# Attention with routing into eight experts: another order of work where the last attention units meet the first expert blocks

## The chip, the cores and the metric

One core of a Trainium2 chip runs one program. The metric is the device time of one execution in microseconds (us). Instructions of the five engines are named PE (TensorE matmul), PEld (TensorE weight load), DVE (VectorE), ACT (ScalarE), POOL (GpSimd) and SP (SyncE, which here only issues DMAs).

## What is computed

Attention with capped scores over 4 batches of 12 heads, 448 rows and 64 columns, then a layer of eight experts in which each of the 1792 rows goes to the one expert with its largest gate logit:

```python
scores = cap * np.tanh(scale * np.matmul(q, k.transpose(0, 1, 3, 2)) / cap)
attn = np.exp(scores - np.max(scores, axis=-1, keepdims=True))
attn = attn / (np.sum(attn, axis=-1, keepdims=True) + 1e-09)
x = np.matmul(attn, v)           # 4 batches, heads side by side: x is 1792 x 768
e_idx = np.argmax(x @ w_gate, axis=1)
gate_w = softmax(x @ w_gate)[np.arange(N), e_idx]
eom = 1 / (1 + np.exp(-(x @ w_output_gate)))
for e in range(8):
    mask = e_idx == e
    h = np.maximum(x[mask] @ w1[e], 0.0)          # 768 x 1024
    out[mask] = gate_w[mask, None] * eom[mask, e, None] * (h @ w2[e])   # 1024 x 768
```

## The kernel before, in words

**Attention.** The work is cut into 24 units, `u` = 0 to 23; a unit is two heads of one batch, six units a batch. A unit has four score steps `qk(u, 0..3)` on PE, each followed on ACT by a tanh (`th`, L302) and an exponential (`pt`, L284). One unit later come the value products `pv(u, 0..3)` (L317, L320) into the PSUM tile `u`, and `u_evac` (L338 on ACT or L340 on DVE, chosen by unit number) copies that to `ut`. The sums of the exponentials are added up by `presum` (L328, L329, L333: `pa`, `pb`), on POOL for units 0 to 21 and on DVE for units 22 and 23; `sums` (L352) then reduces two units at a time over partitions on PE. `t_k` and `t_q` (L271, L258: `tk`, `tq`) turn the keys and queries two units ahead, and DVE makes their low parts `KL`, `QL` (L252).

**End of a batch.** When a batch's units are done, `end_of_batch` normalises, routes and stores its rows: `row_tr(p)` turns a unit's result on PE (`trow`, L483), `row_out(p)` scales it on DVE (`xr`, L487) and sends it to the DRAM tensor `xs`, and `place`, `enter` and so on enter each row's position in the tables `tab`, with an indirect DMA on POOL (L474). The tiles `tk`, `tq`, `trow` and most other turned tiles share one tag of two PSUM buffers (`ps_t`, tag "t"), so that each waits until DVE or ACT has read the tile two before it.

**The seam.** For the first three batches the steps are hung into the score loop by a table of positions (`at`: four positions a unit, counted from the batch's end; for the third batch 7 is the last quarter of unit 20, 9 and 10 lie in unit 21, 15 and 16 in the last quarter of unit 22 and the first of unit 23). `RWP` holds the positions of the rows 1 to 5 of the third batch; row 0 stands at 6. `NXP` holds those of the six steps of `early()`, which work out on DVE, in operations on one partition, which expert (`meta` row 0), whether it changes (row 1) and which table range (row 2) each of the first five expert blocks has. Step 5 is the seven operations from `bval` to the second `meta`, step 6 the four from `bch` to `used`. `fetch_dma(i)` (L733) has SP read four table pieces `tc` for block `i`, `gather(i)` adds them up on POOL (L738 to L741) and fetches the block's 128 rows of `xs` by an indirect DMA (`xg`, L748), and `tx(i)` turns these on PE (`pt_x`, L760), with `xh` and `xl` made by ACT and DVE. `load_raw` (L710) has SP load one 512 KB or 384 KB piece of an expert's weights. The first blocks use only rows of the first three batches.

**Experts.** Blocks 0 and 1 go through the same weights together (`mm_two`), chunk by chunk of 128 input columns; a chunk is six matmuls for each block (L968). Each weight piece is first split by ACT (L946) and DVE (L947) into a high and a low part. The rest of the last batch's routing is a list of steps, `STEPS`, one group taken after each chunk (`step()` in `between`): `g` and `G` are the gate products, `s` reads the sums, `S` turns them, `x`, `X`, `l`, `c`, `r`, `p`, `q`, `e` route, digits are rows, `n` is a step of `late()`, `zh` fetches the next block's tables.

**What sets the order.** The program is written out by hand, and each engine runs its part of it strictly in that order. SP's DMAs use eight semaphores in turn, so that each DMA waits until the eighth before it has landed.

Of the kernel before, what the change touches and what calls it, by code (L numbers as in the profile page):

```python
# [21 lines left out]
def tile_kernel(ctx: ExitStack, tc, q, k, v, cap, w_gate, w_ogate, w1, w2, out):  # L22
    nc = tc.nc
    B, H, S, D = q.shape
# [5 lines left out]
    NU = B * NP  # L30
    REG = 15 * 128
    NTAB = 128 + E * REG
    NSLOT = 18
    NE = 5
# [16 lines left out]
    AH = 6  # L51
    PZ = 4
    RWP = (9, 10, 12, 13, 14)
    NXP = (7, 7, 7, 7, 7, 7)
    F1 = 5
    F2 = 4
    PRE = 3
    STEPS = 'g s S G x0 X1 l2 c rp3 n4 n5 q e n n n n n n zh'
    WARM = (32, 8, 12, 0)
    RB = 7  # L60
    SP0 = 3
# [2 lines left out]
    UACT = 18  # L64
# [269 lines left out]

    def u_evac(u):
        t = utp.tile([128, S], F32, tag="ut", name="ut")
        if UACT <= u < NU - 2 or u == NU - 1:
            nc.scalar.activation(out=t, in_=ups.pop(u), func=ACTF.Copy)  # L338
        else:
            nc.vector.tensor_copy(out=t, in_=ups.pop(u))  # L340
        ut[u] = t

    def sums(u):

        b, p = divmod(u, NP)
        if p % 2 == 0:
            return
        r = p // 2
        if r == 0:
            smt[b] = ps_m.tile([128, S], F32, tag="sm", name="sm")  # L350
        for g in range(4):
            nc.tensor.matmul(smt[b][32 * g:32 * g + 32], lhsT=ohc[:, r, :], rhs=s1[u - 1 + g // 2][:, g % 2],  # L352
                             start=(r == 0), stop=(r == NP // 2 - 1))
# [10 lines left out]
    def end_of_batch(b):  # L364
# [128 lines left out]
        L = lambda *fs: (lambda: [f() for f in fs])  # L493
        P = lambda f, *a: (lambda: f(*a))
# [3 lines left out]
        if b < B - 2:  # L498
            at = {1: [t[2], t[3]], 2: [sums_out], 5: [t[1]], 6: [rws[0]], 9: [gts[0]], 10: [rws[1]], 13: [gts[1]], 14: [rws[2]],
                  15: [logits], 16: [choose], 18: [rws[3]], 21: [rank_mm, place], 22: [rws[4]], 23: [place2], 24: [enter]}  # L500
            at.setdefault(26 if b < B - 3 else 22, []).append(rws[5])
        elif b == B - 2:
            g = early()
            nx = P(next, g, None)
            lds = [P(load_raw, 0, w, c) for w in range(2) for c in range((KD, KF)[w])]
            fd = [P(fetch_dma, i) for i in range(NE)]
            at = {-1: [sums_out], 1: [t[2], t[3]], 2: [t[1], *gts], 3: [logits], 4: [choose],
                  6: [rws[0]], 6.5: [rank_mm, place, place2, enter]}
            for i, x in enumerate(RWP, 1):
                at.setdefault(x, []).append(rws[i])  # L510
            for i, x in enumerate(NXP):
                at.setdefault(x, []).append(nx)
            for x, fs in ((10.5, [fd[0], fd[1], P(set_known, NE), lds[0]]), (15, [P(gather, 0), *lds[1:6], fd[2]]),
                          (16, [P(gather, 1), fd[3], *lds[6:]])):
                at.setdefault(x, []).extend(fs)
        if b < B - 1:
            for x, fs in at.items():
                for f in fs:
                    slots.setdefault(4 * NP * (b + 1) + 4 + x, []).append(f)
            return  # L520
        nx = P(next, late_steps, None)
        do = dict(g=t[2], s=t[0], S=t[1], G=t[3], x=gts[0], X=gts[1], l=logits, c=choose, r=rank_mm, p=place, q=place2,
                  e=enter, n=nx, z=L(P(set_known, NSLOT), P(fetch_dma, NE)), h=lambda: next(rests(), None))
        do.update({str(p): rws[p] for p in range(NP)})
        return [L(*[do[x] for x in w]) for w in STEPS.split()]


    def M(nm, shape):
        return rtp.tile(shape, F32, tag="b" + nm, name="b" + nm)

    def red(o, i, op=ALU.add):
        nc.vector.tensor_reduce(out=o, in_=i, axis=AX.X, op=op)

    def tt(o, x, y, op):
        nc.vector.tensor_tensor(out=o, in0=x, in1=y, op=op)
# [51 lines left out]
    def early():  # L587


        cnt, key, srt, gt = M("cnt", [1, E]), M("key", [1, E]), M("srt", [1, E]), M("le", [1, E, E])  # L590
        cm, nb, nbp, more = M("cm", [1, E]), M("nb", [1, E]), M("nbp", [1, E]), M("more", [1, E])
        g14 = M("g14", [1, E, 14])
        lo, hi = M("lo", [1, 1, E]), M("hi", [1, 1, E])
        tt(cnt, pres[(B - 1) % 2][0:1, 0], ereg, ALU.subtract)

        stt(srt, cnt, float(E), ALU.mult, e8, ALU.subtract)
        ts(cm, cnt, -127.0, ALU.add)
        tt(gt, over(srt, E), srt.unsqueeze(2).to_broadcast([1, E, E]), ALU.is_gt)
        tt(g14, cm.unsqueeze(2).to_broadcast([1, E, 14]), mrow.unsqueeze(1).to_broadcast([1, E, 14]), ALU.is_gt)
        red(key, gt)  # L600
        red(nb, g14)
        yield

        ts(nbp, key, 0.0, ALU.is_equal, 2.0, ALU.mult)
        ts(more, key, float(E - 1), ALU.is_equal, float(NE), ALU.mult)
        tt(nbp, nbp, nb, ALU.max)
        tt(gt, over(key, E), key.unsqueeze(2).to_broadcast([1, E, E]), ALU.is_le)
        tt(nbp, nbp, more, ALU.add)
        yield
        tt(gt, gt, over(nbp, E), ALU.mult)  # L610
        red(hi[:, 0], gt)
        tt(lo[:, 0], hi[:, 0], nbp, ALU.subtract)
        yield
        yield from slots_of(lo, hi, nb, ereg.unsqueeze(1), 0, NE)
# [60 lines left out]
    def rests():  # L675

        full, h, hx, wo = rt["rest"]
        sh = [1, 2, NO, E]
        oh, o2 = M("roh", sh), M("ro2", sh)
        two = lambda x: x.unsqueeze(2).to_broadcast(sh)  # L680
        own = lambda i: metah[:, i, NW:].rearrange("a (z n) -> a z n", z=2)
        tt(wo, wo, over(full, NW), ALU.mult)
        tt(oh, two(hx), irow[:, 0:NO].unsqueeze(1).unsqueeze(3).to_broadcast(sh), ALU.is_equal)
        red(metah[:, 2, 0:NW], wo, ALU.max)
        tt(oh, oh, two(h), ALU.mult)
        tt(o2, oh, full.unsqueeze(1).unsqueeze(1).to_broadcast(sh), ALU.mult)
        red(own(1), oh, ALU.max)
        red(own(2), o2, ALU.max)
        tt(o2, oh, e8.unsqueeze(1).unsqueeze(1).to_broadcast(sh), ALU.mult)
        red(own(0), o2, ALU.max)  # L690
        yield


    tb, xg = {}, {}
# [38 lines left out]
            nc.sync.dma_start(out=t4[:, c], in_=tabs[c][bass.ds(off, 128)])  # L733

    def gather(i):
        t4 = tcs.pop(i)
        t = xgp.tile([128, 2], F32, tag="tb", name="tb", bufs=6)
        nc.gpsimd.tensor_tensor(out=t4[:, 0:2], in0=t4[:, 0:2], in1=t4[:, 2:4], op=ALU.add)  # L738
        nc.gpsimd.tensor_tensor(out=t, in0=t4[:, 0], in1=t4[:, 1], op=ALU.add)
        ti = xgp.tile([128, 1], U32, tag="ti", name="ti", bufs=6)  # L740
        nc.gpsimd.tensor_scalar(out=ti, in0=t[:, 0:1], scalar1=float(NT), scalar2=None, op0=ALU.add)  # L741
        tb[i] = (t, ti)
        n = (B - 1) * S if i < NE else NT + 8
        g = xgp.tile([128, DM], F32, tag="xg", name="xg")
        if i in (1, 3, 4):

            nc.gpsimd.memset(g, 0.0)
        nc.gpsimd.indirect_dma_start(  # L748
            out=g, out_offset=None, in_=xs[0:n], in_offset=bass.IndirectOffsetOnAxis(ap=ti, axis=0),
            bounds_check=n - 1, oob_is_err=i not in (1, 3, 4))  # L750
        xg[i] = g

    def tr_split(src, n, tag, bufs, pool):
        hi = pool.tile([128, n, 128], F32R, tag=tag + "h", name=tag + "h", bufs=bufs)
        lo = pool.tile([128, n, 128], F32R, tag=tag + "l", name=tag + "l", bufs=bufs)
        for a in range(0, n, 4):
            m = min(4, n - a)
            ps = ps_t.tile([128, 4, 128], F32, tag="t", name="pt_" + tag)
            for c in range(m):
                nc.tensor.transpose(ps[:, c], src[:, (a + c) * 128:(a + c + 1) * 128], ident)  # L760
            nc.scalar.activation(out=hi[:, a:a + m], in_=ps[:, 0:m], func=ACTF.Copy)
            nc.vector.tensor_tensor(out=lo[:, a:a + m], in0=ps[:, 0:m], in1=hi[:, a:a + m].bitcast(F32), op=ALU.subtract)
        return hi, lo

    def tx(i):
        if i < NSLOT:
            xg[i] = tr_split(xg[i], KD, "x", 2, xgp)
# [58 lines left out]
    for b in range(B - 1):  # L826
        end_of_batch(b)

    def step():
        if bg:  # L830
            bg.pop(0)()
# [28 lines left out]
    for u in range(NU):  # L860
# [24 lines left out]
        if u > 0:  # L885
            pv(u - 1, 3)
            u_evac(u - 1)
# [8 lines left out]
    u = NU - 1  # L896
# [245 lines left out]

    split_to(SP0)
    bg.extend(end_of_batch(B - 1))
    pv(u, NK)
    u_evac(u)
    tx(0)
    step()
    sums(u)
    step()  # L1150
    gather(2)

    def last_bg():
# [20 lines left out]
    for k in range(NH):  # L1174
        i = SIDES[k][0]
# [69 lines left out]
```

## Time and profile before

| | us |
|---|---|
| median of 3 runs (lowest to highest) | 529.62 (529.43 to 530.06) |
| the profiled execution, its own time | 527.99 |
| its span, first to last instruction | 526.3 |
| PE busy in the span | 508.1 (97%) |
| granted TensorE clock, mean | 0.995 of full speed |
| ACT, DVE, POOL busy | 381.6, 345.5, 298.7 |

PE is busy nearly all the time, so the table says little by itself: what matters is the few stretches in which PE is idle or runs slowly, and what it waits for there. The profile's time is 1.6 us under the median, of which 1.7 us lie around the span.

### The profile page before, as it was taken

The page shows a single profiled execution, that of the slowest core. Times are in us where ns is not written, and L with a number is a line of the kernel's source. Part 1 is how long each engine was busy: PE and PEld are TensorE (multiplying, and loading weights), DVE is VectorE, ACT ScalarE, POOL GpSimd, SP SyncE. Part 2 cuts the span into 40 slices and gives each one's busy share as a digit, 9 for nine tenths or more (in the row PEclk, how much of TensorE's full clock was granted, in tenths as well). Part 3 has the DMA queues.
Part 4 walks back from the last instruction along what each step waited for, and adds up shares of the span by engine and source line. Part 5 has one row for each costly group of instructions (what it writes and reads, how often), then busy time and mean ns, then how long its engine had stood idle before and what let it go on. Part 6 is the DMA issues. An engine that isn't in the chain of part 4 may idle for free. (4 is left out here: it accounts for less than half of the span.)

```text
span 526.3 us, 10342 instructions
## 1 busy us (share of the span) xinstructions
PE 508.1 (97%) x3197; PEld 361.5 (69%) x3197; DVE 345.5 (66%) x576; ACT 381.6 (73%) x498; POOL 298.7 (57%) x341
## 2 busy tenths in 40 slices
PE   7999999999999989699999999999999999999995
PEld 6555465555655544377999898887878968666692
DVE  3363354965496877599998996975758686545460
ACT  5989897888787978535678886886766787555561
POOL 8988967778987696435254975314737015182001
PEclk9999999999999999899999999999999999999999
DMA  6644434445445316887159636329659959994001
GB/s 148 142 108 102 105 74 106 103 108 111 102 113 132 73 36 189 289 303 219 49 184 389 243 95 206 128 69 386 242 169 391 375 173 368 359 349 167 1 31 49
DMA packets 106189, 91.94 MB, mean 175 GB/s; under 512 B 80770, under 2 KB 88970, under 8 KB 106128
## 3 DMA queue, kind: packets, MB, share of 16 engines
q1 hardware_dynamic: 97392, 58.48, 38.2%
q0 software_dynamic: 8736, 32.74, 17.2%
q8 instruction: 27, 0.44, 0.3%
q14 instruction: 34, 0.28, 0.2%
HBM read 123.68 MB, written 12.04 MB: 258 GB/s over the span
## 5 line engine op out<-in xcount | busy, mean ns | idle before, releaser
L947 DVE TENSOR_TENSOR wr<-raw,wr 128x768 fp32r<-128x768 f32 (+1 forms) x167 | 172.0, 1067 | 68.3 <-ACT wr L946 59.4
L946 ACT ACTIVATE wr<-raw 128x768 fp32r<-128x768 f32 (+1 forms) x167 | 150.2, 936 | 33.0 <-DMA raw<-in_moe_w_dram 12.1
L302 ACT ACTIVATE th<-s,icap 128x896 f32<-128x896 f32 x96 | 84.3, 915 | 27.4 <-PE s L297 19.0
L284 ACT ACTIVATE pt<-th,capc 128x896 f32<-128x896 f32 x96 | 85.7, 947 | 0.0
L968 PE MATMUL py<-wr,hh 128*128 128x384 f32 x352 | 77.3, 340 | 0.0
L968 PE MATMUL php<-wr,xh 128*128 128x512 f32 x264 | 74.8, 404 | 0.0
L1037 POOL DMA_INDIRECT out_dram<-yo,ti x13 | 18.5, 1426 | 86.6 <-ACT yo L1035 62.2
L968 PEld LDWEIGHTS py<-wr,hh 128*128 128x128 f32 x352 | 61.2, 188 | 4.0 <-issue 3.7
L317 PE MATMUL u<-pt,vv 128*64 128x448 f32 x288 | 59.4, 548 | 0.5 <-ACT ut L338 0.5
L968 PEld LDWEIGHTS php<-wr,xh 128*128 128x128 f32 x264 | 47.6, 189 | 12.9 <-issue 2.1
L329 POOL TENSOR_TENSOR pb<-pa,pt 128x896 f32<-128x896 f32 x22 | 46.5, 2113 | 17.0 <-issue 13.7
L333 POOL TENSOR_TENSOR pb<-pb,pt 64x448 f32<-64x448 f32 x44 | 52.1, 1185 | 4.5 <-DMA tab<-ent,posi 1.2
L328 POOL TENSOR_TENSOR pa<-pt 128x896 f32<-128x896 f32 x22 | 46.3, 2104 | 2.3 <-ACT ex L439 0.8
L968 PE MATMUL py<-wr,hl 128*128 128x384 f32 x176 | 44.8, 335 | 0.0
L968 PE MATMUL php<-wr,xl 128*128 128x512 f32 x132 | 41.4, 395 | 0.0
L317 PEld LDWEIGHTS u<-pt,vv 128*64 128x64 f32 x288 | 18.5, 136 | 30.5 <-issue 23.1
L1084 POOL DMA_DIRECT2D rh<-in_moe_w_dram x42 | 23.5, 561 | 22.7 <-issue 16.3
L297 PE MATMUL s<-QH,KH 64*128 64x448 f32 x144 | 31.7, 432 | 1.7 <-ACT th L302 1.7
L968 PEld LDWEIGHTS py<-wr,hl 128*128 128x128 f32 x176 | 31.8, 188 | 0.0
L340 DVE COPY ut<-u 128x448 f32<-128x448 f32 x19 | 11.8, 623 | 29.9 <-PE u L320 29.1
L968 PEld LDWEIGHTS php<-wr,xl 128*128 128x128 f32 x132 | 24.7, 187 | 6.0
L1138 POOL DMA_INDIRECT out_dram<-yh,toh x6 | 6.0, 1008 | 38.0 <-ACT wr L946 10.0
(243 smaller groups left out, 862.6 us busy)
## 6 DMA issues: line engine op xcount, KB each, us to landing
raw<-in_moe_w_dram SPq DMA_DIRECT2D x78, 512.0 KB
raw<-in_moe_w_dram SPq DMA_DIRECT2D x104, 384.0 KB
rh<-in_moe_w_dram POOLq DMA_DIRECT2D x18, 512.0 KB
rh<-in_moe_w_dram POOLq DMA_DIRECT2D x24, 384.0 KB
lq<-in_q_dram SPq DMA_DIRECT2D x24, 224.0 KB
kk<-in_k_dram SPq DMA_DIRECT2D x24, 192.0 KB
vv<-in_v_dram SPq DMA_DIRECT2D x24, 192.0 KB
xs<-xr SPq DMA_DIRECT2D x18, 224.0 KB
```

The lines of the kernel that those rows point to most:

```text
L284: nc.scalar.activation(out=dst, in_=th, func=ACTF.Exp, scale=capc)
L297: nc.tensor.matmul(ps[:, j, 0:S], lhsT=x[h, sl], rhs=y[h], start=(i == 0), stop=(i == 2))
L302: nc.scalar.activation(out=th[:, 0:n], in_=ps[:, 0:n, 0:S], func=ACTF.Tanh, scale=icap)
L317: nc.tensor.matmul(ups[u][64 * j:64 * j + 64], lhsT=V[:, c, j, :], rhs=P[:, 2 * c + j], start=(c == 0), stop=False)
L328: eng.tensor_tensor(out=a, in0=P[:, 0:2], in1=P[:, 2:4], op=ALU.add)
L329: eng.tensor_tensor(out=s1[u], in0=a, in1=P[:, 4:6], op=ALU.add)
L333: eng.tensor_tensor(out=s1[u][h, j], in0=s1[u][h, j], in1=P[h, 2 * NK], op=ALU.add)
L946: nc.scalar.activation(out=t[:, 0, 0:F], in_=raw, func=ACTF.Copy)
L947: nc.vector.tensor_tensor(out=t[:, 1, 0:F], in0=raw, in1=t[:, 0, 0:F].bitcast(F32), op=ALU.subtract)
L968: nc.tensor.matmul(ps[g][:, 0:n], lhsT=st[:, c], rhs=w[:, z, g * n:(g + 1) * n], start=(c == 0 and st is hi and z == 0), stop=(c == (KD, K ...
L1037: nc.gpsimd.indirect_dma_start(out=out, out_offset=bass.IndirectOffsetOnAxis(ap=ti, axis=0), in_=y, in_offset=None, bounds_check=NT - 1, o ...
L1084: nc.gpsimd.dma_start(out=d, in_=src[bass.ds(e, 1)].rearrange("e (k p) f -> p (e k) f", p=128)[:, c], **kw)
```

## The change

The diff moves work; no computation is added or dropped. `gather` is split into `index` (the additions) and `take` (the indirect DMA).

```diff
-    NXP = (7, 7, 7, 7, 7, 7)
+    NXP = (7, 7, 7, 7, 9, 10)
-    STEPS = 'g s S G x0 X1 l2 c rp3 n4 n5 q e n n n n n n zh'
+    STEPS = 'g U s S G x0 X1 l2 c 3r p4 n5 n q e nn n n nn zh'
 def u_evac(u):
-        if UACT <= u < NU - 2 or u == NU - 1:
+        if UACT <= u < NU - 3 or u == NU - 1:
 # end_of_batch, third batch
-            for x, fs in ((10.5, [fd[0], fd[1], P(set_known, NE), lds[0]]), (15, [P(gather, 0), *lds[1:6], fd[2]]),
-                          (16, [P(gather, 1), fd[3], *lds[6:]])):
+            for x, fs in ((10.5, [fd[0], P(set_known, NE)]), (11, [lds[0], P(index, 0)]), (14, [fd[1]]),
+                          (15, [P(take, 0), fd[2], *lds[1:4]]), (16, [P(gather, 1), *lds[4:6], fd[3], *lds[6:]]),
+                          (18.5, [P(tx, 0)])):
 # end_of_batch, last batch
-                  e=enter, n=nx, z=...
+                  e=enter, n=nx, U=P(sums, NU - 1), z=...
     def gather(i):
+        index(i)
+        take(i)
+
+    def index(i):
         ...
         tb[i] = (t, ti)
+
+    def take(i):
+        ti = tb[i][1]
         n = (B - 1) * S if i < NE else NT + 8
 # after the loop over units
     pv(u, NK)
     u_evac(u)
-    tx(0)
-    step()
-    sums(u)
     step()
     gather(2)
```

On PE, where attention ends (`vv_129` belongs to unit 22, `vv_130` to unit 23; `php` is chunk 0), before:

```order
L320 MATMUL u<-pt,vv_129 128x448
L317 MATMUL u<-pt,vv_130 64x448 x6
L320 MATMUL u<-pt,vv_130 128x448
L760 MATMUL pt_x<-ident,xg 128x128 x6
L389 MATMUL tg<-ut,wg 32x448 x4
L352 MATMUL sm<-pb,ohc 32x448 x4
L968 MATMUL php<-wr,xh 128x512 x4
L968 MATMUL php<-wr,xl 128x512 x2
```

And now:

```order
L320 MATMUL u<-pt,vv_129 128x448
L768 MATMUL pt_x<-ident,xg 128x128 x6
L317 MATMUL u<-pt,vv_130 64x448 x6
L320 MATMUL u<-pt,vv_130 128x448
L389 MATMUL tg<-ut,wg 32x448 x4
L976 MATMUL php<-wr,xh 128x512 x4
L976 MATMUL php<-wr,xl 128x512 x2
L352 MATMUL sm<-pb,ohc 32x448 x4
```

The turning of the gathered rows now stands ahead of unit 23's value products, and the last sums behind chunk 0.

On DVE, in unit 21, before (from the end of step 5 on):

```order
L535 TENSOR_TENSOR bo_2452<-bo_2452,boh 1x40
L532 TENSOR_REDUCE meta<-bo_2452 1x5
L535 TENSOR_TENSOR bch<-meta 1x4
L532 TENSOR_REDUCE bsm<-boh 1x4
L535 TENSOR_TENSOR meta<-bch,bsm 1x4
L532 TENSOR_REDUCE used<-boh 1x8
L487 TENSOR_TENSOR xr<-trow,rec 112x512 x2
L252 TENSOR_TENSOR KL<-tk,KH 128x512
L252 TENSOR_TENSOR QL<-tq,QH 128x448
```

And now (between the first rows and the last, the middle of step 5 is left out):

```order
L487 TENSOR_TENSOR xr<-trow,rec 112x512
L543 SCALAR_TENSOR_TENSOR bval<-blo,ereg 1x8
...
L536 TENSOR_TENSOR bo_2452<-bo_2452,boh 1x40
L533 TENSOR_REDUCE meta<-bo_2452 1x5
L487 TENSOR_TENSOR xr<-trow,rec 112x512
L536 TENSOR_TENSOR bch<-meta 1x4
L533 TENSOR_REDUCE bsm<-boh 1x4
L536 TENSOR_TENSOR meta<-bch,bsm 1x4
L533 TENSOR_REDUCE used<-boh 1x8
L252 TENSOR_TENSOR KL<-tk,KH 128x512
L252 TENSOR_TENSOR QL<-tq,QH 128x448
```

Step 5 moved from ahead of both rows to between them, step 6 to behind the second row and ahead of `KL`.

On SP, in units 21 to 23, with the semaphores that each DMA waits for (`raw_0` and `raw_1` are the first two weight pieces, `xs` the rows 3 to 5), before:

```order
L710 DMA raw_0_112<-in_moe_w_dram 128x1024 [waits DMAHW5_49]
L110 DMA vv_130<-in_v_dram 128x6x64 [waits DMAHW6_49,PE_49]
L112 DMA vv_130<-in_v_dram 64x64 [waits DMAHW7_49,PE_49]
L112 DMA vv_130<-in_v_dram 64x64 [waits DMAHW0_49]
L490 DMA xs<-xr 448x1x128 [waits DMAHW1_49,DVE_49]
L490 DMA xs<-xr 448x1x128 [waits DMAHW2_49,DVE_49]
L490 DMA xs<-xr 448x1x128 [waits DMAHW3_49,DVE_49]
L710 ISA
L710 DMA raw_1_113<-in_moe_w_dram 128x1024 [waits DMAHW4_49]
```

And now (the four pieces of block 1's table and some register work are left out):

```order
L711 DMA raw_0_112<-in_moe_w_dram 128x1024 [waits DMAHW4_49]
L490 DMA xs<-xr 448x1x128 [waits DMAHW5_49,DVE_49]
L490 DMA xs<-xr 448x1x128 [waits DMAHW6_49,DVE_49]
L490 DMA xs<-xr 448x1x128 [waits DMAHW7_49,DVE_49]
...
L734 DMA tc<-tab_108 128x2 [waits DMAHW4_49]
L734 ISA
L734 DMA tc<-tab_109 128x2 [waits DMAHW5_49]
L734 ISA
L734 DMA tc<-tab_110 128x2 [waits DMAHW6_49]
L734 ISA
L734 DMA tc<-tab_111 128x2 [waits DMAHW7_49]
L711 ISA
L711 DMA raw_1_113<-in_moe_w_dram 128x1024 [waits DMAHW0_49]
```

The pieces 1 to 5 of the first weights, which followed the rows directly, now follow eight table reads of blocks 1 and 2, and the last four of these wait on the semaphores of `raw_0` and the rows.

## Rows read from the trace of the kernel before

**Rows 1.** Stages: us, busy (x count) of five engines, PEclk, DMA share, GB/s

```profile
216.10:220.40 4.30, 4.28 (x23) 1.59 (x24) 1.02 (x2) 1.58 (x4) 1.50 (x4) 0.60 0.45 134
...
400.00:500.00 100.00, 100.00 (x577) 73.39 (x576) 60.82 (x67) 63.56 (x86) 31.91 (x46) 1.00 0.72 268
```

**Rows 2.** PE at the seam: start, us, instruction, idle before and releaser

```profile
208.33 2.48 PE L317 MATMUL u<-pt,vv 128*64 128x448 f32 x12
210.74 1.02 PE L320 MATMUL u<-pt,vv 128*128 128x448 f32 x2
216.12 0.85 PE L760 MATMUL pt_x<-ident,xg 128*128 128x128 f32 x6 [4.36 <-DMA xg<-xs,ti]
216.89 1.72 PE L389 MATMUL tg<-ut,wg 128*32 128x448 f32 x8
218.38 1.73 PE L352 MATMUL sm<-pb,ohc 128*32 128x448 f32 x8
220.03 1.32 PE L968 MATMUL php<-wr,xh 128*128 128x512 f32 x4
221.66 0.60 PE L372 MATMUL trec<-ident,ssb 128*112 128x128 f32 x4
```

**Rows 3.** PE, the same forms at full clock elsewhere

```profile
205.08 0.96 PE L352 MATMUL sm<-pb,ohc 128*32 128x448 f32 x8
```

**Rows 4.** SP: start, us of issuing, DMA and count

```profile
203.06 1.98 SPq L490 DMA_DIRECT2D xs<-xr  x3
205.26 3.31 SPq L710 DMA_DIRECT2D raw<-in_moe_w_dram  x5
```

**Rows 5.** POOL, units 20 to 23

```profile
190.77 2.09 POOL L329 TENSOR_TENSOR pb<-pa,pt 128x896 f32<-128x896 f32 x1
192.94 2.35 POOL L333 TENSOR_TENSOR pb<-pb,pt 64x448 f32<-64x448 f32 x2
195.37 2.11 POOL L328 TENSOR_TENSOR pa<-pt 128x896 f32<-128x896 f32 x1
199.74 4.33 POOL L333 TENSOR_TENSOR pb<-pb,pt 64x448 f32<-64x448 f32 x2
209.00 1.14 POOL L748 DMA_INDIRECT xg<-xs,ti  x1 [3.43 <-DMA raw<-in_moe_w_dram]
```

**Rows 6.** DMA queues in 209.0 to 213.0: packets, MB, share of 16 engines

```profile
q1 hardware_dynamic: 393, 1.45, 98.3%
```

**Rows 7.** DVE, PE and ACT in units 21 and 22

```profile
187.14 0.15 DVE L542 SCALAR_TENSOR_TENSOR bval<-blo,ereg 1x8 f32<-1x8 f32 x1
188.67 2.04 DVE L535 TENSOR_TENSOR meta<-bch,bsm 1x4 int32<-1x4 f32 x1
190.77 1.27 DVE L487 TENSOR_TENSOR xr<-trow,rec 112x512 f32<-112x512 f32 x2
...
186.88 0.65 PE L483 MATMUL trow<-ident,ut 128*112 128x128 f32 x4
...
192.09 0.60 PE L258 MATMUL tq<-ident,lq 112*128 112x112 f32 x4
...
194.35 0.65 PE L483 MATMUL trow<-ident,ut 128*112 128x128 f32 x4 [0.25 <-DVE KL L252]
...
189.63 1.53 ACT L302 ACTIVATE th<-s,icap 128x896 f32<-128x896 f32 x2 [2.80 <-PE s L300]
```

**Rows 8.** DVE, then POOL, in another batch's end

```profile
149.84 2.15 DVE L542 SCALAR_TENSOR_TENSOR cand<-d,iota 112x32 f32<-112x32 f32 x1
...
149.83 2.11 POOL L328 TENSOR_TENSOR pa<-pt 128x896 f32<-128x896 f32 x1
```

**Rows 9.** DVE in unit 22

```profile
200.02 1.08 DVE L328 TENSOR_TENSOR pa<-pt 128x896 f32<-128x896 f32 x1
```

**Rows 10.** PE's waits from 220 to the end: us in total, times, longest

```profile
PE trow L483 <- DVE bcm L542: 0.7, 1, 0.7
```

**Rows 11.** PE's wait in unit 23

```profile
202.68 2.48 PE L317 MATMUL u<-pt,vv 128*64 128x448 f32 x12 [0.53 <-ACT ut L338]
```

More of the change, by code (lines that the diff above doesn't have):

```diff
@@ L522, in end_of_batch @@
         do = dict(g=t[2], s=t[0], S=t[1], G=t[3], x=gts[0], X=gts[1], l=logits, c=choose, r=rank_mm, p=place, q=place2,
-                  e=enter, n=nx, z=L(P(set_known, NSLOT), P(fetch_dma, NE)), h=lambda: next(rests(), None))
+                  e=enter, n=nx, U=P(sums, NU - 1), z=L(P(set_known, NSLOT), P(fetch_dma, NE)), h=lambda: next(rests(), None))
         do.update({str(p): rws[p] for p in range(NP)})
```

## The prediction

> **What bounds the kernel now.** I read the stages first: from 400 to 500 us PE is busy all the time at full clock [rows 1], and it is so over nearly the whole expert part. There a start that is earlier by one us ends the kernel one us earlier, so the change is worth what it moves the point at which the expert part gets going. As that mark I take the end of chunk 0, 221.66 in PE's rows [rows 2], with turned rows, unit 23's value products, the gate products of one group and the last sums done.
>
> PE's rows at the seam show what is lost ahead of the mark. PE ends unit 23's value products at 211.76 and waits 4.36 us for the gathered rows `xg` [rows 2]. Behind the wait it runs slowly: the granted clock is 0.60 of full on the mean of 216.1 to 220.4 [rows 1], a mix of its two levels, 2.4 and 1.2 GHz, and the sums take 1.73 us [rows 2] against 0.96 at full clock in unit 22 [rows 3].
>
> Why `xg` is late stands in three views. SP issued rows 3 to 5 only from 203.06 to 205.04, and the weights right behind [rows 4]; POOL's gather waited 3.43 us, until 209.00 [rows 5]; and from 209.0 to 213.0 all the moved bytes were on the queue of the weights, which filled 98.3% of the DMA engines [rows 6]. So the gather, issued by 210.14, moved nothing before 213.0 and landed by 216.12: 3.1 us once it had its turn.
>
> **The change part by part.** Sums are made against the profiled run (527.99 us of its own, 526.3 of span); it lies 1.6 us under the median of 529.62, and I put differences onto the median.
>
> *PE's order.* At full clock the work from 208.33 to the mark is: value products 3.43 (208.33 to 211.76), the turning 0.77, gate products 0.8 (from the slow 1.72, scaled as the sums are, 0.96/1.73, this gives 0.95; the step from start to next start was 1.49, which gives 0.83), chunk 0 1.6, sums 0.9: together 7.5 [rows 2, 3]. With no stall the mark is at 208.33 + 7.5 = 215.8, or 5.8 earlier. The moves of `tx(0)` and of the sums add nothing; they let 3.4 us of value products stand behind the turning, so ACT and DVE have these to split `xg` in. The price: PE in order now waits for `xg` ahead of the value products, where before these 3.4 us of work covered some of the wait.
>
> *DVE's order.* Before, steps 5 and 6 ran from 187.14 on ahead of both rows, and `xr` only began at 190.77 [rows 7]. Now row 1's `xr` comes first, at 187.5 to 188.2 (its turn on PE ends at 187.53, and one `xr` is half of 1.27 [rows 7]). Then step 5 comes, no longer under a free POOL but under POOL's sums, which run without a gap from 190.77 to 195.29 and from 195.37 to 197.48 [rows 5], and already before. The trace shows twice what a DVE operation from SBUF can cost there: the last of step 6 took 2.04 us on 1x4 elements, until POOL's next sum started, against 0.15 for the first of step 5 [rows 5, 7]; and one on 112x32 that began 10 ns behind a POOL sum of 2.11 took 2.15 [rows 8]. But the other way is there too: a DVE addition of 1.08 at 200.02 ran at once, and POOL's two sums took 4.33 instead of 2.35 [rows 5, 9]. So the price of step 5 lies between seven times 0.15, about 1, and one POOL sum for each operation that takes its operands from SBUF and depends on the one ahead, of which four can wait. I take three waits, nearest to the two rows of 2 us: to 190.7, 192.9 and the middle of the pair at 194.1. Row 2's `xr` then ends at 195.05, and `tq`, which shares its two buffers, starts there instead of at 192.09. Step 6's two operations wait to 195.3 and 197.48, `KL` follows, and row 3's turn, which needs the buffer of `tk`, starts at 198.4 instead of 194.35 [rows 5, 7]: 4.05 later, all of it on PE's path, since the rows behind stand in PE's order.
>
> The Trainium skill speaks against this move: "Trainium Architecture — The Big Picture", section "What this means for kernel authors", says that VectorE and GpSimd share a port pair as an exclusive lock and not as a split of bandwidth, and "GPSIMD Engine Reference", section "Key points", names instructions with two SBUF inputs. The trace agrees in the two rows of 2 us [rows 7, 8], and shows with the pair of 4.33 that the lock may fall to either engine [rows 5, 9]. By the lock alone each of the waits above is a POOL sum; were the port shared evenly, the step would cost about 1 to 2.
>
> *`ut(21)` on DVE.* PE waited 0.53 for ACT's copy [rows 11]; DVE is free then, so I take 0.53 off, between 0 and 0.53. The delay is 4.05 - 0.53 = 3.5.
>
> *SP and POOL.* Rows 3 to 5 no longer stand behind eight table reads, so they go as soon as `xr` is made. POOL's next stop for the gather is its own sums, which end at 199.74 + 4.33 = 204.07 [rows 5]; 1.14 of issue and 3.1 of flight give a landing at 208.3, or 211.8 with the 3.5. The additions of `index` were moved to unit 21 or 22 and cost nothing on PE's path; POOL's sums are later by them, under 1 us by their place. The weight loads now wait, by the eight semaphores, for `raw_0` and the rows; they come about with the gather. They are wanted by chunk 1 on, and DMA had room in 216.1 to 220.4 (0.45 busy [rows 1]): I cost that at 0 to 1.
>
> *The rest of the list.* The sums a chunk later, and the list's order, should halve the one later wait of 0.7 on `trow` [rows 10] or remove it: 0 to -0.7, taken as -0.5 with what a half clock at the mark leaves behind.
>
> *Sum.* PE comes to the turning at 208.33 + 3.5 = 211.8, the gather lands at 211.3 to 212.3: wait 0.2. The mark is at 215.8 + 3.5 + 0.2 = 219.5, against 221.66: -2.1. With -0.5: -2.6, or 529.62 - 2.6 = **527.0**. A wait more or less of step 5 (2.1), and half of one for the loads, give the own range, 525.4 to 528.6.
>
> **The rivals.**
>
> *Steps 5 and 6 cost little.* POOL is the one that waits, as at 200.02 [rows 9], or DVE's short operations slip between. The turning starts at 208.3, when both PE and gather are there, the mark is at 215.8: -5.8 - 0.5 = -6.3, **523.3**. For it: one clear row, and the four 0.15s of step 5 need only a gap each. Against: two rows [rows 7, 8].
>
> *They cost all.* ACT's tanh at 189.63 had waited 2.80 for PE [rows 7], though PE's rows of that time are done earlier; if PE's rows are recorded too early here, row 1's `xr` is only at 189.6 to 190.2, four operations wait until 197.48, and row 3's turn is near 200.7: +6.4. PE then idles some 7 us in units 21 and 22, with half clock behind it at 0 to 1.5. The stall at the seam is gone, and 215.8 + 6.4 + 0.7 + up to 1.5 for the late gather is about 222.9 to 224.4, less 0.5: -0.5 to +2.5, middle **530.3**.
>
> *The gather is late, and PE in order waits ahead of the value products* (the other side). With the landing at L the mark is L + 7.5 (turning, value products, gate, chunk, sums); it breaks even at 221.66 - 7.5 = 214.2. If loads still overtake the gather and it lands as before, at 216.12, the mark is 223.6: +2, **531.6**. For it: the loads filled the DMA engines for 4 us ahead of an issued gather [rows 6], and `fd[2]` with the first loads is listed right behind `take(0)`, on another engine's queue, so that nothing makes them wait for the gather itself, only for the rows. In that sense the change may not do what it says. Against: the rows land just when POOL can issue, and a load needs SP to first issue four table reads.
>
> The Trainium skill, "DMA: Bandwidth & Descriptors", section "Queues, rings and completion order", has each DMA engine go round-robin between queues packet by packet. By it the gather could not wait behind loads, and the last rival would fall away; the trace differs, with no packet of the gather in 4 us [rows 6], so I let the row decide.
>
> **How the numbers follow.** Chances: part given back 0.42 (527.0), steps cheap 0.25 (523.3), steps cost all 0.20 (530.3), gather late 0.13 (531.6). The prediction is the first. The range, 522.8 to 530.8, takes in the cheap case with half a us to spare and half of the costly one; it leaves out about 0.2, above all at the top. A measurement of this kernel can tell about 0.2% (1.06 us) from no change: faster is below 528.56, all of the cheap case, nine tenths of the first, and little else: 0.66. Within 0.2%: the rest of the first, and half of the costly case: 0.18. Slower, above 530.68: the rest of both rivals: 0.16.
>
> **What would show it.** In the profile after: DVE's step 5 and 6 at 2 us a piece with POOL's sums beside them (first case), or 0.15 each (second); `tq` at 195 and row 3's turn at 198.4, or 192 and 194; PE's wait for `xr` in unit 21 at 1.2 plus about 3, and none at `ut(21)`; rows 3 to 5 issued as soon as made, and the gather waiting for POOL and not for a DMA; packets of the gather's queue soon behind its issue; the turning of `xg` without a wait ahead of unit 23's value products; the clock at 1.00 behind it, and the sums at 0.96. The prediction is wrong if PE is held in units 21 and 22 by something else (a buffer, `ut`, DVE's copies), or if the weights, now later, are waited for in chunks 1 to 5.

## The result, and the profile after

The changed kernel took 534.45 us (median of 7 runs, 532.29 to 538.47), the kernel before 529.99 us beside it: a ratio of 1.0097, 95% interval 1.0073 to 1.012. It is slower by about 1%, where 0.5% faster was forecast. The profiled run took 535.11 us (span 533.4), 7.12 us more than that of before; the medians are only 4.46 us apart, so an account of these two executions explains more than the typical loss.

Stages of the changed kernel (us, busy time and count of PE, PEld, DVE, ACT, POOL, granted clock, DMA share, GB/s):

```profile
195.00:200.00 5.00, 4.85 (x22) 3.36 (x24) 4.08 (x8) 2.75 (x4) 4.61 (x3) 0.53 0.23 47
210.00:220.00 10.00, 7.21 (x43) 3.21 (x39) 7.50 (x15) 7.01 (x10) 5.37 (x10) 1.00 0.83 284
...
250.50:254.50 4.00, 3.96 (x11) 3.13 (x12) 1.53 (x8) 0.00 (x0) 0.67 (x1) 0.57 0.51 177
```

The half clock of the seam [rows 1] is gone, as the 1.00 of 210 to 220 shows. But two other stretches now run near 1.2 GHz: 195 to 200, behind a stop of PE in unit 21, and 250.5 to 254.5, behind a stop in block 2.

PE's rows with a wait in the changed kernel (start, us, instruction, idle before and releaser):

```profile
195.15 1.01 PE L258 MATMUL tq<-ident,lq 112*128 112x112 f32 x4 [4.30 <-DVE xr L487]
198.62 1.10 PE L483 MATMUL trow<-ident,ut 128*112 128x128 f32 x4
...
213.77 0.88 PE L768 MATMUL pt_x<-ident,xg 128*128 128x128 f32 x6 [1.24 <-DMA xg<-xs,ti]
...
219.55 0.96 PE L389 MATMUL tg<-ut,wg 128*32 128x448 f32 x8 [1.55 <-ACT ut L338]
...
222.03 0.96 PE L352 MATMUL sm<-pb,ohc 128*32 128x448 f32 x8
222.92 1.20 PE L976 MATMUL php<-wr,xh 128*128 128x512 f32 x4
...
242.59 0.44 PE L768 MATMUL pt_x<-ident,xg 128*128 128x128 f32 x2 [1.64 <-DVE xl L770]
...
250.54 0.47 PE L976 MATMUL ph<-wr,xh 128*128 128x512 f32 x1 [2.43 <-DVE ble L536]
```

The mark of the prediction (turning, value products, gate group 0, sums and chunk 0 done) is at 222.92, where it was at 221.66 [rows 2]: not 2.1 earlier but 1.26 later. Behind it stand two waits that were not there, 1.64 and 2.43, for the 0.7 of before [rows 10] and a 0.3. From 250.5 to 254.5 the clock was 0.57, so that block 2's first twelve matmuls took 4.41 us (250.54 to 254.95), against 2.79 before (245.75 to 248.54): 1.6 more. Mark 1.3, waits 3.1 and half clock 1.6 make 6.0 of the 7.1 us; the rest was not followed.

### The profile page after: what moved, and what is told of

Its sections match the earlier page's. It is cut to its first block, busy times and chain, and to the rows that moved or that the text cites. A ratio compares the mean times of both kernels' runs of the same rounds, so it can differ in the third digit from the quotient of the medians.

```text
span 533.4 us, 10339 instructions
## 1 busy us (share of the span) xinstructions
PE 510.5 (96%) x3197; PEld 363.3 (68%) x3197; DVE 350.6 (66%) x577; ACT 382.0 (72%) x497; POOL 290.3 (54%) x341
## 5 line engine op out<-in xcount | busy, mean ns | idle before, releaser
L333 POOL TENSOR_TENSOR pb<-pb,pt 64x448 f32<-64x448 f32 x44 | 50.1, 1138 | 4.0 <-DMA tab<-ent,posi 0.7
L474 POOL DMA_INDIRECT tab<-ent,posi x16 | 15.6, 974 | 24.1 <-DVE ent L472 14.5
```

The lines of the kernel that those rows point to most:

```text
L333: eng.tensor_tensor(out=s1[u][h, j], in0=s1[u][h, j], in1=P[h, 2 * NK], op=ALU.add)
```

## The experiments

The kernels named a_ start from the changed kernel, those named b_ and l_ from the kernel before, c_ and d_ lead to a third one. The runs were taken in four sets: first a_list, a_nxp, a_list_nxp and b_list; then c_tx, d_split, b_nxp and b_tx; then d_nxp, l_rp, l_row5 and p_none; last the repeats and a_split. Ratios are to runs of the kernel before in the same set. Diffs are short; each leaves out what only follows from it.

**Undo one part, or two.** The list of steps and the last sums of before in the changed kernel (a_list), steps 5 and 6 back ahead of the rows (a_nxp), and both.

```diff
# a_list
-    STEPS = 'g U s S G x0 X1 l2 c 3r p4 n5 n q e nn n n nn zh'
+    STEPS = 'g s S G x0 X1 l2 c rp3 n4 n5 q e n n n n n n zh'
     u_evac(u)
     step()
+    sums(u)
+    step()
     gather(2)
# a_nxp
-    NXP = (7, 7, 7, 7, 9, 10)
+    NXP = (7, 7, 7, 7, 7, 7)
```

> The changed kernel with the list of steps and the last sums as they were before (sums ahead of chunk 0, 'rp3 n4 n5', one step fewer of delay); everything else as changed. Theory (the list is the larger half of the loss): of the 1.64 us wait of the turned rows of block 2, the 2.43 us wait of block 2's first matmul and the half clock behind it (1.6) none is left, and the 0.7 and 0.3 of before come back: about 4.7 us off the changed kernel's 534.45, 529.5 to 530.5, or 0.999 to 1.001 of before. Rival (the waits behind the seam come from the later weights, and the list only shows them): within 1 us of the changed kernel, 1.008 to 1.010 of before.

> The changed kernel with steps 5 and 6 back ahead of the rows 1 and 2; everything else as changed. Theory (DVE's waits for POOL's sums cost 4.1 us on PE's path, and 0.5 of half clock behind): PE reaches the turning of block 0's rows near 208 instead of 212.5; the gather, no longer held back by the rows, lands 3 to 4 us earlier than 213.8; 3 to 4.5 us off the changed kernel, 530 to 531.5, 1.000 to 1.003 of before. Rival (the gather and the weights set the seam, not PE's arrival): PE waits for the gather as much longer as it comes earlier, 533.5 to 534.5, 1.007 to 1.009.

> Both edits at once: the list of before and steps 5 and 6 of before, with the order of SP and POOL, the turning ahead of unit 23's value products and the copy by DVE as changed. Theory (the two losses add, and the rest of the change is a gain): 525 to 527, 0.990 to 0.995 of before. Rival (the rest of the change is worth nothing, since ACT's copy of unit 23 then waits behind the weights): 529 to 530.5, 0.998 to 1.002.

Measured: a_list 534.25 us, 1.0083 (1.0054 to 1.0112); a_nxp 533.95 us, 1.0083 (1.0057 to 1.0108); both together 529.30 us, 0.9999 (0.998 to 1.0018). Each alone gave nearly nothing, both gave 5 us. a_list_nxp missed its theory: the rest of the change is worth nothing, as the rival said, but not for the rival's reason. PE's wait for ACT's copy was 0.63 us there; what took the gain was PE's wait of 3.93 us for the gather, with value products of 4.17 us behind it. For a_nxp the rows at the seam say why (PE):

```profile
207.24 0.91 PE L320 MATMUL u<-pt,vv 128*128 128x448 f32 x2
212.07 1.54 PE L768 MATMUL pt_x<-ident,xg 128*128 128x128 f32 x6 [3.92 <-DMA xg<-xs,ti]
213.54 4.21 PE L317 MATMUL u<-pt,vv 128*64 128x448 f32 x12
```

PE comes 4.4 us earlier to the turning (208.15 for 212.53), but the gather lands only 1.7 us earlier. PE waits 3.92 us, with unit 23's value products queued behind that wait, and these then take 4.21 us for 2.48, at half clock (0.55 over 212.0 to 217.7). So most of what unit 21 gave back went at the seam: the expectation's theory was wrong there and its rival nearly right. In a_list both later waits were gone, as expected, but the time was not: its unit 21 looked worse than the changed kernel's, a wait of 7.39 us for 4.30. That is taken up below.

**The list alone, on the kernel before.**

> The kernel before with the new list of steps alone (and the last sums a chunk later). Theory (the list by itself makes both waits: 'r' and 'p' in two steps keep one of the two turned buffers while block 2's rows are turned, and row 5 comes two chunks later, in the bank of block 2's first matmul): waits of 1.6 and 2.4 and half clock behind them, less the 1.0 of before: 3.5 to 5.5 slower, 533 to 535.5, 1.007 to 1.011 of before. Rival (the waits need the late weights too): 529 to 531, 0.999 to 1.003.

Measured: 533.38 us, 1.0075 (1.0048 to 1.0102). The two waits are there to the hundredth, without the later weights or any other part of the change:

```profile
242.94 0.44 PE L760 MATMUL pt_x<-ident,xg 128*128 128x128 f32 x2 [1.65 <-DVE xl L762]
...
250.90 0.47 PE L968 MATMUL ph<-wr,xh 128*128 128x512 f32 x1 [2.43 <-DVE ble L535]
```

The half clock behind the second is not: PE's clock stayed at 1.00 here, as it did in after_again and a_split below, so that it is no fixed part of the list's price. The stage behind the wait in b_list:

```profile
250.90:254.90 4.00, 4.00 (x22) 3.36 (x23) 1.50 (x7) 0.49 (x1) 0.67 (x1) 1.00 0.51 186
```

**What the two waits are.** Two variants of b_list, one run each.

```diff
# l_rp
-    STEPS = '... c 3r p4 n5 n q e ...'
+    STEPS = '... c 3 rp4 n5 n q e ...'
# l_row5
-    STEPS = '... l2 c 3r p4 n5 n q e ...'
+    STEPS = '... l2 c3 4r p5 n n q e ...'
```

> As b_list (the kernel before with the new list), with the rank products 'r' in one step with 'p', which reads them, a chunk later than in the change. Theory (in the change, 'r' holds one of the two turned buffers over the turning of block 2's rows): the wait of 1.65 us of the second half of these rows (near 241 us) is gone, the wait of 2.43 us of block 2's first matmul stays. Rival (that wait is the weights' or DVE's load, whatever the buffers): both stay.

> As b_list, with the rows 3, 4 and 5 of the last batch one step earlier ('c3 4r p5 n n' for 'c 3r p4 n5 n'). Theory (row 5's turned tile lies in the PSUM bank of block 2's first matmul, and its copy by DVE stood behind six small operations): the wait of 2.43 us of block 2's first matmul is gone, with the half clock behind it, and the wait of 1.65 stays. Rival (block 2's first matmul waits for its weights): both stay.

Measured: 530.85 us and 530.11 us (single runs). PE in l_rp, then in l_row5:

```profile
239.25 0.82 PE L760 MATMUL pt_x<-ident,xg 128*128 128x128 f32 x6
...
247.94 0.47 PE L968 MATMUL ph<-wr,xh 128*128 128x512 f32 x1 [2.30 <-DVE ble L535]
```

```profile
238.36 0.65 PE L483 MATMUL trow<-ident,ut 128*112 128x128 f32 x4 [1.12 <-DVE xr L487]
242.85 0.44 PE L760 MATMUL pt_x<-ident,xg 128*128 128x128 f32 x2 [1.48 <-DVE xl L762]
247.76 0.39 PE L968 MATMUL ph<-wr,xh 128*128 128x512 f32 x1
```

Each edit took away the wait that it was made for and left the other (l_row5 has a new one of 1.12, for row 3's turn). So the first wait is one of buffers: the rank products `trk` hold one of the two turned buffers until `p` reads them; with `r` and `p` in different steps the turning of block 2's rows, which stands between, has a single buffer left, and its second half waits until DVE has read the first. The second is one of a bank: in the last batch `row_tr` takes its tile from the tag `hph`, and so does block 2's first matmul. DVE's rows of the changed kernel show how late the reader of that tile is:

```profile
248.59 0.15 DVE L543 SCALAR_TENSOR_TENSOR bcm<-pre,ereg 1x8 f32<-1x8 f32 x1
...
249.70 0.69 DVE L487 TENSOR_TENSOR xr<-trow,rec 112x512 f32<-112x512 f32 x1
250.31 0.20 DVE L536 TENSOR_TENSOR ble<-lek,bnb 1x64 f32<-1x64 f32 x1
```

Row 5's `xr` ends at 250.39 and the matmul starts at 250.54; the profile names the operation that DVE had begun by then. In the kernel before this `xr` was done near 242.7, three microseconds ahead of block 2. The new list has one entry more in front (`U`) and one `step()` fewer ahead of chunk 0, so that row 5 is taken two chunks later.

**The turning ahead of the value products.** On the kernel before alone (b_tx), and taken back in a_list_nxp (c_tx).

```diff
# b_tx
-                          (16, [P(gather, 1), fd[3], *lds[6:]])):
+                          (16, [P(gather, 1), fd[3], *lds[6:]]), (18.5, [P(tx, 0)])):
     u_evac(u)
-    tx(0)
```

> The kernel before with the turning of block 0's rows ahead of unit 23's value products, alone. The gather lands near 216 as before. Theory (PE in order holds 3.4 us of value products behind the wait): PE waits about 7.8 us instead of 4.4, and the value products run at half clock behind it: end of chunk 0 at 224.5 to 226 instead of 221.7: 3 to 4.5 us slower, 533 to 534.5, 1.005 to 1.009 of before. Rival (the value products only change places with the splitting of the rows, for which PE waits anyway): within 1 us of before.

> As a_list_nxp (the list of before, steps 5 and 6 of before, the changed order of SP and POOL, unit 21's copy by DVE), but the turning of block 0's rows is back behind unit 23's value products. In a_list_nxp PE reached the turning at 208.2 and waited 3.9 us for the gather, with 3.4 us of value products standing behind that wait and running at half clock after it. Theory (the new place of the turning is a loss as long as the gather lands after 211.6): the wait shrinks to about 0.5 us, no half clock, the end of chunk 0 comes at 216 to 218 instead of 221.8: 3.5 to 5.5 us off a_list_nxp's 529.3, 524 to 526, 0.988 to 0.993 of before. Rival (ACT's copy of unit 23 behind the late weights, and the splitting of the turned rows, take it back): 527.5 to 529.5, 0.995 to 1.000.

Measured: b_tx 532.83 us, 1.0052 (1.0036 to 1.0068): a loss by itself, as expected. PE in b_tx:

```profile
215.83 1.51 PE L760 MATMUL pt_x<-ident,xg 128*128 128x128 f32 x6 [7.91 <-DMA xg<-xs,ti]
217.28 4.07 PE L317 MATMUL u<-pt,vv 128*64 128x448 f32 x12
```

c_tx took 528.37 us, 0.9967 (0.9954 to 0.998): better than before, but 2 to 4 us short of the theory. PE, then ACT, in c_tx:

```profile
211.36 0.88 PE L767 MATMUL pt_x<-ident,xg 128*128 128x128 f32 x6 [0.77 <-DMA xg<-xs,ti]
216.58 1.72 PE L389 MATMUL tg<-ut,wg 128*32 128x448 f32 x8 [4.34 <-ACT ut L338]
```

```profile
213.02 1.06 ACT L953 ACTIVATE wr<-raw 128x1024 fp32r<-128x1024 f32 x1 [4.27 <-DMA raw<-in_moe_w_dram]
215.04 1.06 ACT L953 ACTIVATE wr<-raw 128x1024 fp32r<-128x1024 f32 x1 [0.96 <-DMA raw<-in_moe_w_dram]
216.00 0.53 ACT L338 ACTIVATE ut<-u 128x448 f32<-128x448 f32 x1
```

The wait for the gather is 0.77 and the rest of the rival came true: ACT stands before two weight splits whose weights now land behind the gather, with unit 23's copy queued behind them, and PE waits 4.34 us for that copy. The stall of the seam had only changed its name.

**The copy ahead of the weight splits.** In c_tx (d_split) and in the changed kernel itself (a_split).

```diff
-    split_to(SP0)
     bg.extend(end_of_batch(B - 1))
     pv(u, NK)
     u_evac(u)
     tx(0)
+    split_to(SP0)
```

> As c_tx, and the first two weight splits of ACT and DVE stand behind unit 23's copy and the splitting of the turned rows instead of ahead of them. Theory (ACT's copy of unit 23 waits for weights that land after the gather): PE's wait for that copy (0.6 in a_list_nxp, 1.55 in the changed kernel) goes and the turned rows are split at once: 0.5 to 1.5 us faster than c_tx, 523 to 525.5. Rival (the two splits, now later, are waited for by chunks 1 and 2): as c_tx or up to 1 us slower.

> The changed kernel with the first two weight splits behind unit 23's copy on ACT, the rest as changed. Theory (ACT's copy waits for weights that now land after the gather, and PE waits for the copy 1.55 us): that wait falls to 0.6 us and the end comes about 1 us earlier than the changed kernel's of this set. Rival (chunk 1 then waits for its weights): the same time as the changed kernel.

Measured: d_split 525.28 us, 0.9916 (0.9895 to 0.9938), the fastest of all and 3.1 us under c_tx, more than expected. a_split 533.94 us, 1.0071 (1.0052 to 1.0089), against 1.0091 (1.0061 to 1.0122) for the changed kernel of the same set: its wait for `tg` is 0.63, but the difference in time is within the intervals, and the changed kernel's own profile of that set, after_again, has 0.69 there instead of 1.55: there was hardly a wait to take away. PE in d_split:

```profile
212.00 0.88 PE L767 MATMUL pt_x<-ident,xg 128*128 128x128 f32 x6 [1.01 <-DMA xg<-xs,ti]
212.80 0.96 PE L389 MATMUL tg<-ut,wg 128*32 128x448 f32 x8
213.58 0.93 PE L352 MATMUL sm<-pb,ohc 128*32 128x448 f32 x8
214.44 1.20 PE L975 MATMUL php<-wr,xh 128*128 128x512 f32 x4
```

The sums take 0.93 and not 1.73 [rows 2]; chunk 0 is done near 216.1, 5.6 us earlier than before [rows 2].

**Steps 5 and 6 alone.** Their move on the kernel before (b_nxp), in d_split (d_nxp), and the changed kernel with POOL's sums cut short (p_none).

```diff
# b_nxp, d_nxp
-    NXP = (7, 7, 7, 7, 7, 7)
+    NXP = (7, 7, 7, 7, 9, 10)
# p_none, in presum
+        m = 8 if u == 20 or (u, s) == (21, 0) else S
...
+            if m < S:
+                nc.gpsimd.memset(s1[u], 1.0)
-            eng.tensor_tensor(out=a, in0=P[:, 0:2], in1=P[:, 2:4], op=ALU.add)
+            eng.tensor_tensor(out=a[:, :, 0:m], in0=P[:, 0:2, 0:m], in1=P[:, 2:4, 0:m], op=ALU.add)
```

> The kernel before with steps 5 and 6 moved to between and behind the rows 1 and 2, alone. Theory (each dependent operation waits for a sum of POOL, and rows, gather and weights move with PE): PE waits 4.3 to 7.4 us for DVE in unit 21 and runs at half clock behind it, and the stall at the seam stays, since the gather waits for the rows: 4 to 8 us slower, 534 to 538, 1.008 to 1.015 of before. Rival (the gather keeps its time, and the stall of 4.4 us at the seam takes the delay up): 530 to 532, 1.000 to 1.004.

> As d_split, with steps 5 and 6 where the change put them (between and behind the rows 1 and 2). Before, that move alone cost 0.2% only, since the stall at the seam took up most of it. Theory (in d_split only 1 us of stall is left there, and the gather moves with the rows, so that nothing takes the delay up): PE waits 3.3 to 7.4 us for DVE in unit 21, part of it at half clock behind, and the end comes 3 to 7 us later than d_split's 525.28: 528.5 to 532, 0.997 to 1.004 of before. Rival (a slack elsewhere takes it up again): within 1 us of d_split.

> The changed kernel, in which POOL's sums of the exponentials of unit 20, and those of unit 21 but the last, are made of 8 columns of 448 only (the rest is set to one), so that POOL has 0.2 us operations in place of 2.1 there; the rows of these units get wrong weights, and what comes behind unit 22 is not read. Theory (DVE's small operations wait for POOL's sums): the operations of steps 5 and 6 take 0.15 to 0.25 us each, none 1 to 2 us, and PE's wait of 4.3 us for unit 23's queries shrinks to 0.3 to 1.3 us. Rival (they wait for something else on their way, ACT or a semaphore): 1 to 2 us each, as in the changed kernel.

Measured: b_nxp 530.68 us, 1.0019 (1.0005 to 1.0033): the rival. d_nxp 533.21 us, 1.0061 (1.004 to 1.0083), against 0.9916 without the move, in another set: the theory, and above its range, with 7.45 us of wait in unit 21. That set is one with late signals (below); the changed kernel waits 4.3 us there in the other sets, so about 3 of the 7.9 us between d_nxp and d_split may belong to the set, by this estimate. b_nxp's waits tell the difference (PE):

```profile
194.36 1.01 PE L258 MATMUL tq<-ident,lq 112*128 112x112 f32 x4 [3.32 <-DVE xr L487]
...
218.24 0.85 PE L760 MATMUL pt_x<-ident,xg 128*128 128x128 f32 x6 [1.92 <-DMA xg<-xs,ti]
219.01 0.96 PE L389 MATMUL tg<-ut,wg 128*32 128x448 f32 x8
```

A wait in unit 21 of 3.32 for 1.23 at this place before, then 1.92 for 4.36 [rows 2] at the seam, and no half clock behind it. The stall of the seam was slack for what came ahead of it; once d_split had removed it, the same move cost at least the wait that it makes, 7.45 for 1.25.

In p_none, which is read in unit 21 only, DVE did this with POOL's long sums gone, and PE's wait for `tq` behind it was 1.23 us, as expected (DVE's rows, then PE's):

```profile
191.26 0.19 DVE L539 TENSOR_TENSOR boh<-boh,bo 1x40 f32<-1x40 f32 x1
191.48 0.19 DVE L546 SCALAR_TENSOR_TENSOR bo<-irow,bval 1x40 f32<-1x40 f32 x1
191.70 0.19 DVE L539 TENSOR_TENSOR bo<-bo,boh 1x40 f32<-1x40 f32 x1
...
192.76 0.60 PE L258 MATMUL tq<-ident,lq 112*128 112x112 f32 x4 [1.23 <-DVE xr L490]
```

and this in the changed kernel, with POOL's sums behind it:

```profile
188.79 2.13 DVE L536 TENSOR_TENSOR boh<-boh,bo 1x40 f32<-1x40 f32 x1
190.96 2.12 DVE L543 SCALAR_TENSOR_TENSOR bo<-irow,bval 1x40 f32<-1x40 f32 x1
193.11 1.17 DVE L536 TENSOR_TENSOR bo<-bo,boh 1x40 f32<-1x40 f32 x1
...
188.77 2.10 POOL L328 TENSOR_TENSOR pa<-pt 128x896 f32<-128x896 f32 x1
190.95 2.07 POOL L329 TENSOR_TENSOR pb<-pa,pt 128x896 f32<-128x896 f32 x1
193.10 2.32 POOL L333 TENSOR_TENSOR pb<-pb,pt 64x448 f32<-64x448 f32 x2
```

0.19 for 2.1, and 1.23 of wait where a_list, the same kernel up to there and in a set of the same kind (below), had 7.39: POOL's sums are the cause.

**The same kernels once more.** Why a_list alone had gained nothing.

> The changed kernel once more, in one set with the two others. What differs from set to set is when the signals of row 1's turn reach DVE and ACT (ACT's tanh in unit 21 after a wait of 1.5 or of 2.8 us): with the early signals PE waits 4.3 us for unit 23's queries and the time is 532 to 535, with the late ones 7.4 us and 537 to 539.

> The changed kernel with the list and the last sums of before, in one set with the changed kernel. Theory (the list costs the changed kernel what it costs the kernel before, and its first set was one of late signals): 3.5 to 5.7 us faster than the changed kernel of this set, waits of 1.64 and 2.43 gone. Rival (behind the stalls of the seam the list costs nothing): within 1 us of it.

Measured, in one set: the changed kernel 534.62 us, 1.0091; a_list_again 529.07 us, 0.9981 (0.9966 to 0.9996): the list costs the changed kernel 5.5 us. The profile of after_again has the early signals and a wait of 4.29 us for unit 23's queries, and its time is as expected for these. Since a_list_nxp, with steps 5 and 6 put back too, had 0.9999, no loss but the list's is seen when the signals are early, as far as two sets can be compared: what unit 21 costs is then taken up at the seam. The same code as a_list took 534.25 us in its first set. ACT and PE in unit 21, of a_list, then of a_list_again:

```profile
190.66 1.53 ACT L302 ACTIVATE th<-s,icap 128x896 f32<-128x896 f32 x2 [2.86 <-PE s L300]
...
199.38 1.01 PE L258 MATMUL tq<-ident,lq 112*128 112x112 f32 x4 [7.39 <-DVE xr L487]
```

```profile
188.71 1.01 ACT L302 ACTIVATE th<-s,icap 128x896 f32<-128x896 f32 x1 [1.53 <-PE s L297]
...
195.31 0.91 PE L258 MATMUL tq<-ident,lq 112*128 112x112 f32 x4 [4.28 <-DVE xr L487]
```

In some sets of runs the signals of PE's work in unit 21 reach ACT and DVE some 2 us late, by the profile. Then row 1's `xr` starts 2 us later, one operation more waits for a POOL sum, and PE waits 7.4 us for 4.3. That accounts for what a_list had left open; no edit tested it.

## Why the prediction was wrong

**Units 21 and 22: right.** Three waits of step 5 were forecast, to 190.7, 192.9 and 194.1; they ended at 190.92, 193.08 and 194.28. `tq` was forecast at 195.05 and came at 195.15, row 3's turn at 198.4 and came at 198.62; there is no wait for `ut(21)` any more [rows 11]. The forecast holds for the early signals, which the profile read here happened to have. The Trainium skill's rule that spoke against this move ("Trainium Architecture — The Big Picture", section "What this means for kernel authors": VectorE and GpSimd share a port pair as an exclusive lock) agrees with p_none: 0.19 us without POOL's sums, up to 2.13 with them.

**The gather: a term too small.** Forecast to land at 211.3 to 212.3, it landed at 213.77. The flight was right (issued by 210.64, 3.1 us). The step that failed is the one that let POOL's own sums release it, at 204.07 plus the delay. They ended at 204.11, and the gather did not start. SP's and POOL's rows of the changed kernel:

```profile
203.11 2.30 SPq L490 DMA_DIRECT2D xs<-xr  x3
...
209.50 1.14 POOL L756 DMA_INDIRECT xg<-xs,ti  x1 [5.39 <-DMA tc<-tab]
```

POOL was idle 5.39 us. The gather followed SP's first issue of these rows by 6.39 us here, by 5.94 before [rows 4, 5], by 6.41 in a_list_nxp (200.65 and 207.06), and by 6.31 in p_none, where POOL's sums were cut short; over all runs it is 5.8 to 6.5, but for after_again with 7.2. So it follows the rows and not POOL's sums: what releases it is the landing of three 224 KB transfers, and the prediction had given that no time. (The profile puts the wait down to a table read here, and to the rows in a_nxp, c_tx, b_nxp and after_again.) Cost: 1.04 of extra wait, and 0.7 more for PE's later arrival, since the half clock behind the stop in unit 21 had no term.

**"The moves of `tx(0)` and of the sums add nothing": wrong.** The price was even named behind it, PE in order ahead of the value products, but set to 0.2. b_tx measures it on the kernel before, 0.52%. The move has a second price that was not named: nothing is left between unit 23's value products and the gate products, so that PE also waits for ACT's copy of unit 23, 0.63 us in b_tx, where before the turning stood in between.

**"I cost that at 0 to 1", of the later weights: the wrong engine.** I looked at PE's chunks, which want the weights, and not at ACT, where two splits that wait for them stand ahead of unit 23's copy. ACT in the changed kernel:

```profile
216.77 1.06 ACT L954 ACTIVATE wr<-raw 128x1024 fp32r<-128x1024 f32 x1 [1.44 <-DMA raw<-in_moe_w_dram]
...
218.97 0.53 ACT L338 ACTIVATE ut<-u 128x448 f32<-128x448 f32 x1
```

PE waits 1.55 us for that copy here and 4.34 in c_tx; with the splits behind the copy (a_split) 0.63 is left. But the wait changes from run to run: after_again, the same kernel, has 0.69. The instruction to follow is the one that waits first in any engine's order, not the one that uses the data.

With these the mark is explained: 0.7 (arrival) + 1.0 (gather) + 1.55 (copy) = 3.3 of the 3.4 us between 219.5 and 222.92 in this profile.

**"The list's order should halve the one later wait": the step that failed most.** -0.5 was taken, with bounds of 0 and -0.7; it cost 1.64 + 2.43 - 1.0 of wait and 1.6 of half clock, 4.7, in this profile. In medians it is 3.4 us on the kernel before (b_list, where the clock held behind the second wait) and 5.5 by a_list_again. I counted the waits that the old list had and did not place the new list's tiles in their buffers. Both losses could have been read from the code: which tile holds which of the two buffers while the turning of block 2 runs, and which chunk is the last ahead of block 2's use of `hph`. A reordering has no bound of zero on its loss side.

**The rivals.** "They cost all" was the case in other sets (7.4 us of wait), and its guess that row 1's turn is signalled late was right for those (`xr` at 190.59 in a_list). "The gather is late" was half true: PE waited, but 1.24 us, and for the rows' landing, not for weights ahead of the gather. The slower sign came from none of them: it came from a part that had been given one answer.

**Gather and weights.** The prediction let the rows decide against the round robin of the Trainium skill, "DMA: Bandwidth & Descriptors", section "Queues, rings and completion order". The runs bear that out: with weights queued ahead the gather's packets waited again in b_nxp (issued by 211.99, landed at 218.24, 6.3 us), where 324 of the 325 packets of the stretch 212 to 215 were on the weights' queue:

```profile
q1 hardware_dynamic: 324, 1.18, 100.7%
```

Without weights ahead the flight was 3.1 us. A rival cause is DVE's work beside the gather. b_tx speaks against it: its gather was issued by 210.02 and moved no packet before 213, while DVE was idle for 9 us:

```profile
217.59 1.02 DVE L762 TENSOR_TENSOR xl<-pt_x,xh 128x512 fp32r<-128x512 f32 x2 [9.00 <-ACT xh L761]
```

So that part of the change does what it says, and it is the part that d_split keeps.

## What to carry over

A stall late in an ordered program is slack for all that comes ahead of it: a cost placed there hardly shows (b_nxp, 0.2%) until the stall is removed (d_nxp, 1.5% over d_split, part of it perhaps from late signals), and a gain placed there gives nothing back (a_nxp). When a load is moved later, go through each engine's order for the first instruction that waits for it, and see what is queued behind; moving two splits behind one copy was worth 3.1 us of 528 from c_tx to d_split, though nothing clear of noise in the changed kernel. And before a list of steps is shifted, write down for each tile which buffer it takes and who must have read the one before.

## What was not expected of the hardware

By the profile, signals of PE's work came late in whole sets of runs: in the first and third set every profile shows ACT's tanh of unit 21 waiting 2.7 to 2.9 us for PE, in the second and fourth 1.5, with PE's own rows of that time at the same distance from each other. The profile of the kernel before has 2.80, that of the changed kernel 1.53. The medians of the kernel before lie between 529.62 and 530.17 in the four sets, so that it seems to cost nothing there, where other work stands in its place; a_list and a_list_again, the same code, are 5.2 us apart. Two of the changed kernel's first seven runs, 537.64 and 538.47, may be of the late kind, but no trace of them is kept. Whether the signals are late or PE's rows stand too early in the profile is not shown, and the cause stays open.

A stop of PE can cost more than its length: behind 4.30 us (unit 21) the clock was 0.53 over 195 to 200, near its lower level of 1.2 GHz, behind 2.43 us (block 2) 0.57 over 4 us, whereas the stretch from 210 to 220, with stops of 1.24 and 1.55, stayed at 1.00. This price is not fixed: behind the same 2.43 us it was 0.65 over 4 us in a_nxp, and 1.00 in b_list, after_again and a_split. What decides between them is not shown.
